# Rearranging the first microseconds of a fused attention and feed-forward kernel: smaller first tiles, weight loads meant to start earlier, split q, more engines for the casts

## The chip, the cores and the metric

The kernel runs on one core of a Trainium2 chip. The metric is the device time of that core in microseconds (us). Engines are written PE or TensorE (matrix products), PEld (its weight loads), DVE or VectorE, ACT or ScalarE, POOL or GpSimd, SP or SyncE. L603 means line 603 of the kernel in question; the changed kernel is some twenty lines longer, so the same statement has another number there.

## The reference

```python
# q, k, v: [8 batches, 8 heads, 576 tokens, 64]
phi(x) = concat(relu(x) * cos(theta_s), relu(x) * sin(theta_s))
kv  = einsum('bhsf,bhsd->bhfd', phi(k), v);   z = sum over s of phi(k)
num = einsum('bhsf,bhfd->bhsd', phi(q), kv);  den = einsum('bhsf,bhf->bhs', phi(q), z) + 1e-6
x = (num / den) as [4608 tokens, 512]
h = x @ w_in          # 512 x 2048
out = (h * cos(h)) @ w_out   # 2048 x 512
```

All inputs and the output are float32; the products run in float16 with float32 sums.

## The kernel before

Each batch gives 512 tokens to one chunk (four tiles of 128), and the ninth chunk collects the remaining 8 x 64. A planner in the Python code, run when the kernel is built, lists every step with an estimated cost and picks an order for each engine by list scheduling and rounds of random search with a fixed seed. The order is then frozen: at run time an engine executes its list and waits on semaphores. The parts that the change and the argument touch:

```python
# loads of q, k, v: two transfers each, four and five tokens per partition
def load(b, nm, due, hs=(slice(0, H),)):
    m, n = raw[nm], b % 2
    for h in hs:
        ...
        def go5(h=h, five=five):
            nc.sync.dma_start(out=blocks(m, n)[:, h], in_=five)          # partitions 2p + n
        def go4(h=h, four=four):
            nc.sync.dma_start(out=blocks(m, 1 - n)[:, h, 0:NT, :], in_=four)  # partitions 2p + 1 - n
        pl.add("SP", 0.65, 0, due, go4, (), [(x, 1 - n) for x in part], ...)  # issued first
        pl.add("SP", 0.65, 0, due, go5, (), [(x, n) for x in part], ...)      # issued second

# weight loads start only when k of batch 0 has landed: a tiny copy writes into w_in's tile
def weights():
    def hold():
        nc.gpsimd.tensor_copy(
            out=w_in_sb[0:1, 0, :].rearrange("p (g f) -> p g f", g=4)[:, :, 0],
            in_=raw[ORDER0[1]][0:1, 0, 0, 0:1].broadcast_to((1, 4)))     # ORDER0[1] is "k"
    pl.add("POOL", 0.4, 0.5, 0, hold, hk(ORDER0[1]), [("w_in", g) for g in range(4)])
    for g in range(4):      # four quarters of w_in, then w_out, by GpSimd's DMA
        ...

# first layer of chunks 0 and 1: two output blocks x two token tiles in each task
if c < 2:
    for quarter in range(4):
        for hf in range(2):
            for jp in range(2):
                ...   # 8 matmuls of 256 columns, needs x tiles 2*hf and 2*hf + 1
                pe(2 * NCT, MMH, due, mm, xk[2 * hf:2 * hf + 2] + [("w_in", quarter)], [("M1", m)])
                gate(...)          # ScalarE: cos; VectorE: h * cos(h)

FAST1 = {3: 2, 4: 2, 5: 2, 6: 2, 7: 4, 8: 4}   # groups of the first layer with fewer products

def first_attention():
    warm(14, 6.5)                               # dummy matmuls
    for nm in ORDER0:                           # "qkv"; only v in head halves
        load(0, nm, 0, HALVES if nm == ORDER0[2] else (slice(0, H),))
    weights()
    ...                                         # q: relu, transposes
    warm(10, 2.5, [("TR", 0)])
    ...                                         # k: relu; v casts; kv
    for t in range(NT):
        num(0, t, 8 + t, PAIRS[t])
        x_pe(0, t, t, *BANKS[t], "ACT", 8 + t)  # transposes of x and ScalarE's copy
```

A dummy or filler matmul multiplies zeros and only keeps TensorE busy. Batch 1's loads of q, k and v, and the second half of w_out, queue behind w_in and the first half of w_out.

Of the kernel before, what the change touches and what calls it, by code (L numbers as in the profile page):

```python
# [17 lines left out]
class Plan:  # L18
# [10 lines left out]

    PASSES, ROUNDS = 12, 97  # L30

# [78 lines left out]
    def forward(self, key):  # L110
# [27 lines left out]
        def first(n, e, t):  # L138
            opts = st[n]["opts"]
            return len(opts) == 1 or all(  # L140
                t + opts[e][1] <= max(free[x], avail[n]) + o[1] for x, o in opts.items())
        rings, now = {r: [] for r in self.SHARE}, 0.0
# [118 lines left out]
def kernel(  # L261
# [88 lines left out]
    PAIRS = [(BANKS[0], BANKS[1]), (BANKS2[0], BANKS2[1]), None, (BANKS[2], BANKS[3])]  # L350
    PAIRS1 = (None, PAIRS[3])

    Q_PE, X_PE = (), range(1, 3)
    VCAST = ("DVE", "ACT")
    LAZY = 8.0
    LATE_BY, LATE_W = (0.0, 1.0, 3.0, 1.0), 0.6
    ORDER0, ORDER1, HOLDW, W_FIRST = "qkv", "kqv", 1, None
# [9 lines left out]
    def pe(n, cost, due, fn, rd, wr):  # L367
        pl.add("PE", n * cost, n * cost, due, fn, rd, wr)
# [54 lines left out]
    def cast_v(b, t, eng, due, hs=slice(0, H), nt=1):  # L423
        heads = range(H)[hs]
        out_, in_ = V1[:, t, hs, 0:D], raw["v"][:, hs, t, :]
        if nt > 1:
            out_ = V1[:, t:t + nt, :, 0:D].rearrange("p t h d -> p h t d")
            in_ = raw["v"][:, :, t:t + nt, :]
        rd, wr = hk("v", heads), [("V1", t + i, h) for h in heads for i in range(nt)]
        f = nt * len(heads) / H  # L430
        cost = {"DVE": 0.09 + 0.33 * f, "ACT": 0.12 + 0.5 * f, "POOL": 0.9}
        fn = {"ACT": lambda: nc.scalar.activation(out=out_, in_=in_, func=AF.Copy),  # L432
              "DVE": lambda: nc.vector.tensor_copy(out=out_, in_=in_),
              "POOL": lambda: nc.gpsimd.tensor_copy(out=out_, in_=in_)}
        either(due, {e: cost[e] for e in ([eng] if eng else VCAST)}, fn, rd, wr)

# [101 lines left out]

    def x_pe(b, t, n, bank, key, eng, due):
        dst, dkey = xdst(b, t)  # L540
        ps = bank.bitcast(F16)[:, 0:NCT * P].rearrange("p (c s) -> p c s", c=NCT)
        x2 = x16[n].rearrange("p h d -> p (h d)")

        def mm():
            for c in range(NCT):
                nc.tensor.matmul(ps[:, c, :], lhsT=x2[:, c * P:(c + 1) * P], rhs=IDENT,  # L546
                                 is_transpose=True)
        pe(NCT, MMT, due, mm, [("x16", n), "ID"], [key])
        if eng == "ACT":
            act(0.5, due, lambda: nc.scalar.activation(out=dst, in_=ps, func=AF.Copy), [key], [dkey])  # L550
        else:
            dve(0.4, due, lambda: nc.vector.tensor_copy(out=dst, in_=ps), [key], [dkey])
# [10 lines left out]
    def mul(due, cost, fn, rd, wr, pool):  # L563

        if pool is None:
            dve(cost, due, lambda: fn(nc.vector), rd, wr)
        elif pool:
            pl.add("POOL", 0.1 + 2.1 * cost, 0.25 + 2.1 * cost, due, lambda: fn(nc.gpsimd), rd, wr,
                   port=True)
        else:  # L570
            dve(cost, due, lambda: fn(nc.vector), rd, wr, port=True)
# [11 lines left out]
    def layer1(c):  # L583
# [3 lines left out]
        if c < 2:  # L587
            n = 0
            for quarter in range(4):
                for hf in range(2):  # L590
# [50 lines left out]

    FAST1 = {3: 2, 4: 2, 5: 2, 6: 2, 7: 4, 8: 4}
    SUMS_AT = min(FAST1) - 1
# [315 lines left out]

    def warm(n, us, rd=()):  # L960
        def go():
            for i in range(n):
                nc.tensor.matmul(ATT[:, 0, :], lhsT=WZ[:, 0:P], rhs=WZ, start=True, stop=True)
        pl.add("PE", us, us, -1, go, rd, [("ATT", 0)])

    def weights():
        def hold():
            nc.gpsimd.tensor_copy(
                out=w_in_sb[0:1, 0, :].rearrange("p (g f) -> p g f", g=4)[:, :, 0],
                in_=raw[ORDER0[1]][0:1, 0, 0, 0:1].broadcast_to((1, 4)))  # L970
        pl.add("POOL", 0.4, 0.5, 0, hold, hk(ORDER0[1]), [("w_in", g) for g in range(4)])
        for g in range(4):
# [33 lines left out]
    def first_attention():  # L1006
# [4 lines left out]
        for nm in ORDER0:  # L1011
            load(0, nm, 0, HALVES if nm == ORDER0[2] else (slice(0, H),))
        weights()
        for t in range(NT):
            prep(0, "q", t, 0, "DVE", t)
            prep(0, "q", t, 1, "DVE" if t == 1 else "ACT", t)
            q_pe(0, t, *BANKS[t], "ACT" if t % 2 else "DVE", t)
        warm(10, 2.5, [("TR", 0)])
        for t in range(NT + 1):
            prep(0, "k", t, 0, "DVE", 4)  # L1020
            prep(0, "k", t, 1, "DVE" if t == 2 else "ACT", 4)
        for hb in range(2):
            for t in range(NT + 1):
                cast_v(0, t, "ACT" if t % 2 else "DVE", 5 + hb, HALVES[hb])
        kv(0, 7, BANKS2)
        for t in range(NT):
            num(0, t, 8 + t, PAIRS[t])
            x_pe(0, t, t, *BANKS[t], "ACT", 8 + t)

# [109 lines left out]
```

## Time and profile before

| | before |
|---|---|
| times of the first measurement | 283.74, 284.98, 285.03, and one of 722.17 us |
| profiled run (the one of 285.03), span | 283.2 us |
| TensorE busy | 270.7 us, 96% |
| first weight load issued | 11.21 us |
| last part of batch 1's v landed | 43.3 us |
| first layer of batch 1 begins (chain of waits) | 52.47 us |
| last block of 128 products begins | 264.74 us |

The run of 722.17 us is a lone outlier and is left out below. The last four rows are the ones to compare between kernels: they mark where the head ends and where the end is fixed. In the prediction are this kernel's totals, its slices and its timeline around 20 us. The chain of waits, followed back from the last instruction (start in us, length, what), adds the way there:

```profile
2.89 7.76 DMA km<-in_k_dram
...
15.98 0.44 DVE kvz L459
...
52.47 0.87 PE M L603 x8
...
264.74 14.11 PE M L896 x128
```

The reader sees one transfer in the head, k, and after 16.42 us (kvz copied) only the on-chip engines. No load of batch 1 stands on this chain. That is true, and I think it misled the prediction: a load that arrives just in time doesn't show on a chain.

### The profile page before, as it was taken

To read this page: it belongs to the slowest core of one execution; us is meant where nothing else is said; L and a number is where in the kernel's file an instruction comes from. 1 tells how busy PE (TensorE), PEld (TensorE's weight loads), DVE (VectorE), ACT (ScalarE), POOL (GpSimd) and SP (SyncE) were. 2 spreads that over 40 slices of the span, in tenths; PEclk is the share of its full clock that TensorE was granted. 3 is DMA by queue.
4 is the path that set the end of the run, shared out by engine and by line. 5 is a ranking of instruction groups with operands and counts; after the bars stand their busy time and mean duration, and the time that the engine had idled before them with its cause. 6 is when DMAs were issued, how large, how long until landed. Compare 5 with 4: busy or idle time off the path is not lost.

```text
span 283.2 us, 6709 instructions
## 1 busy us (share of the span) xinstructions
PE 270.7 (96%) x2652; PEld 213.6 (75%) x2652; DVE 253.0 (89%) x465; ACT 219.8 (78%) x374; POOL 38.5 (14%) x61
## 2 busy tenths in 40 slices
PE   7669999999999999999999999999999999999993
PEld 2457857677976678787878788868787888888882
DVE  2885798999999999999999999999999999999942
ACT  2944798888999999999999999998554748867610
POOL 1412110020100011001100200020002403331600
PEclk9986999999999999999999999999999999999999
DMA  6999999769998979996998799969032200300124
GB/s 211 304 205 274 254 300 319 243 176 269 270 307 165 316 114 355 247 267 161 285 258 220 170 280 260 242 200 154 0 58 93 87 9 3 148 2 0 68 83 148
DMA packets 77566, 53.29 MB, mean 188 GB/s; under 512 B 46048, under 2 KB 75232, under 8 KB 77536
## 3 DMA queue, kind: packets, MB, share of 16 engines
q1 hardware_dynamic: 70032, 39.73, 59.0%
q0 software_dynamic: 6784, 12.59, 16.8%
q10 hardware_dynamic: 720, 0.57, 0.6%
q8 instruction: 20, 0.33, 0.5%
q14 instruction: 10, 0.08, 0.1%
HBM read 36.74 MB, written 9.44 MB: 163 GB/s over the span
## 4 chain that ended last, share of the span: by engine, by line
PE 85%; DVE 8%; DMA 3%; issue 2%; ACT 1%; SPq 0%; DVEq 0%
PE M L896 32%; PE M L635 12%; PE M L739 11%; PE M L603 9%; PE M L833 5%; PE TR L739 5%; PE ATT L506 3%; PE ATT L445 3%; DMA km<-in_k_dram 3%; PE TR L635 2%; DVE KQ L419 2%; DVE gT L578 1%; DVE km L696 1%; PE M L546 1%; DVE S L878 1%
## 5 line engine op out<-in xcount | busy, mean ns | idle before, releaser
L896 PEld LDWEIGHTS <-gT 128*128 128x128 f16 x560 | 54.0, 98 | 8.4
L578 DVE TENSOR_TENSOR gT<-M,ch 128x512 f16<-128x512 f32 x78 | 51.9, 684 | 6.4 <-ACT ch L576 6.2
L896 PE MATMUL M<-w_out_sb,gT 128*128 128x256 f16 x448 | 56.1, 273 | 0.0
L576 ACT ACTIVATE ch<-M 128x512 f32<-128x512 f32 x80 | 46.7, 596 | 10.5 <-PE M L603 5.8
L418 ACT ACTIVATE KQ<-qm,CS 128x512 f16<-128x512 f32 x59 | 39.9, 721 | 4.4 <-DMA qm<-in_q_dram 4.4
L802 POOL DMA_DIRECT2D out_dram<-ost x32 | 17.6, 554 | 172.1 <-ACT ost L907 80.2
L635 PE MATMUL M<-xT,w_in_sb 128*128 128x512 f16 x160 | 39.0, 379 | 0.0
L418 ACT ACTIVATE KQ<-km,CS 128x512 f16<-128x512 f32 x54 | 37.1, 718 | 0.2 <-DMA km<-in_k_dram 0.2
L603 PE MATMUL M<-xT,w_in_sb 128*128 128x256 f16 x256 | 32.2, 283 | 1.2 <-ACT xT L550 0.7
L896 PE MATMUL M<-T,S 128*128 128x256 f16 x256 | 32.2, 273 | 0.0
L603 PEld LDWEIGHTS <-w_in_sb 128*128 128x128 f16 x256 | 25.7, 102 | 5.7 <-issue 1.8
L907 ACT ACTIVATE ost<-M 128x512 f32<-128x512 f32 x31 | 18.4, 594 | 14.8 <-PE M L896 14.7
L635 PEld LDWEIGHTS <-w_in_sb 128*128 128x128 f16 x192 | 18.2, 98 | 15.0
L896 PEld LDWEIGHTS <-S 128*128 128x128 f16 x256 | 24.9, 98 | 3.7 <-DVE S L878 0.2
L739 PEld LDWEIGHTS <-w_in_sb 128*128 128x128 f16 x240 | 23.0, 98 | 3.9 <-issue 0.2
L526 DVE TENSOR_TENSOR x<-ATT,rec 128x512 f16<-128x512 f32 x31 | 21.4, 691 | 1.1
L911 DVE TENSOR_TENSOR ost<-M,ost 128x512 f32<-128x512 f32 x24 | 16.4, 682 | 3.8 <-issue 3.6
L751 DVE TENSOR_TENSOR Z<-M,Z 128x512 f32<-128x512 f32 x26 | 17.4, 683 | 1.3 <-PE M L739 1.1
L506 PEld LDWEIGHTS <-qT 128*128 128x128 f16 x320 | 15.0, 98 | 4.7 <-issue 1.3
L878 DVE TENSOR_TENSOR S<-gT 128x2048 f16<-128x2048 f16 (+1 forms) x16 | 17.4, 1087 | 0.2
L739 PEld LDWEIGHTS <-WS 128*128 128x128 f16 x144 | 13.8, 98 | 2.4 <-issue 0.5
L432 ACT ACTIVATE V<-vm 128x1024 f16<-128x1024 f32 (+2 forms) x21 | 14.8, 739 | 0.0
(146 smaller groups left out, 461.8 us busy)
## 6 DMA issues: line engine op xcount, KB each, us to landing
out_dram<-ost POOLq DMA_DIRECT2D x32, 256.0 KB, 4.4
qm<-in_q_dram SPq DMA_DIRECT2D x8, 640.0 KB, 7.0
km<-in_k_dram SPq DMA_DIRECT2D x8, 640.0 KB, 6.2
qm<-in_q_dram SPq DMA_DIRECT2D x8, 512.0 KB, 5.9
km<-in_k_dram SPq DMA_DIRECT2D x8, 512.0 KB, 7.7
vm<-in_v_dram SPq DMA_DIRECT2D x6, 640.0 KB, 6.5
vm<-in_v_dram SPq DMA_DIRECT2D x6, 512.0 KB, 7.3
w_in_sb<-in_moe_w_in_dram POOLq DMA_DIRECT2D x4, 512.0 KB, 8.6
```

What stands on the lines that cost most here:

```text
L418: fn = {"ACT": lambda: nc.scalar.activation(out=out_, in_=in_, func=AF.Relu, scale=sc), "DVE": lambda: nc.vector.tensor_scalar(out=out_, i ...
L506: nc.tensor.matmul(bank[hb][:, hh * D1:(hh + 1) * D1], lhsT=a[:, h, :], rhs=z[:, h, :], start=(i == 0), stop=(i == len(parts) - 1))
L526: nc.vector.tensor_tensor(out=split(x16[n][:, hs, :], k), in0=A[:, :, :, 0:D], in1=split(rec[n][:, hs], k).unsqueeze(3).broadcast_to((P, k ...
L576: act(0.5, due, lambda: nc.scalar.activation(out=ch[c], in_=bank, func=AF.Sin, bias=math.pi / 2.0, scale=1.0), [key], [("ch", c)])
L578: mul(due, 0.61, lambda q: q.tensor_tensor(out=dst, in0=bank if len(dst.shape) == 2 else bank.rearrange("p (j s) -> p j s", j=dst.shape[1] ...
L603: nc.tensor.matmul(M1[m][:, jj * 2 * P:(jj + 1) * 2 * P], lhsT=w_in_sb[:, cc, j * P:(j + 1) * P], rhs=X[:, cc, ts], start=(cc == 0), stop= ...
L635: nc.tensor.matmul(M, lhsT=w_in_sb[:, cc, j * P:(j + 1) * P], rhs=X[:, cc, :], start=(cc == 0), stop=(cc == NCT - 1))
L739: nc.tensor.matmul(bank[0][:, j * TH:(j + 1) * TH], lhsT=a(cc, j), rhs=b[:, cc, :], start=(first and j == 0 and cc == 0), stop=(last and j ...
L802: pl.add(eng, 0.9 if eng == "POOL" else 0.65, 0, due, lambda: q.dma_start(out=dst, in_=src_), keys, [], dma=(nb, 355.0))
L878: dve(0.07 + 1.07 / NG, due, lambda: nc.vector.tensor_tensor(out=out_[:, sl], in0=a[:, sl], in1=b[:, sl], op=op), rd, wr, port=True)
L896: nc.tensor.matmul(bank[0][:, tt * MH:(tt + 1) * MH], lhsT=a[:, j, tt * P:(tt + 1) * P], rhs=b[:, j, :], start=(first and tt == 0 and j == 0),
L907: act(0.5, due, lambda: nc.scalar.activation(out=dst, in_=view(bank), func=AF.Copy), [bank[1]], dk)
```

## The change

The intent: begin the dense work sooner. The first layer of batch 0 starts by single token tiles; fillers keep TensorE's clock up meanwhile; the weight loads wait only for k's first part plus a short delay; q comes in head halves so that its preparation can begin early; v's casts may also go to GpSimd; and the last chunk uses two fast groups instead of four. The planner may now also choose the engine for batch 0's preparations of q and k and its casts of v, and has new cost estimates for GpSimd. Because the order is searched anew, every engine's order changes too. The diff cut to its core, without those choices and estimates:

```diff
-    PASSES, ROUNDS = 12, 97
+    PASSES, ROUNDS = 12, 117
...
+    PAIRS0, PAIRS1 = (None, PAIRS[1]), (None, PAIRS[3])
+    QV0 = "qv"
+    FILL = (4, 3, 2, 0)
-    VCAST = ("DVE", "ACT")
+    VCAST = ("DVE", "ACT", "POOL")
-    LATE_BY, LATE_W = (0.0, 1.0, 3.0, 1.0), 0.6
+    LATE_BY, LATE_W = (0.0, 1.0, 3.0, 2.5), 0.6
...
-            for quarter in range(4):
+            for t in range(NT if c == 0 else 0):
+                ...      # 16 matmuls of 128 columns on tile t, quarter 0 of w_in
+                pe(4 * NCT, MMT, due, mm, [xk[t], ("w_in", 0)], [("M1", m)])
+                gate(M1[m], ("M1", m), G[:, 0:4, ts], ...)
+            for quarter in range(1 if c == 0 else 0, 4):
...
-    FAST1 = {3: 2, 4: 2, 5: 2, 6: 2, 7: 4, 8: 4}
+    FAST1 = {3: 2, 4: 2, 5: 2, 6: 2, 7: 4, 8: 2}
...
+    HP = P // 2
...
-                out=w_in_sb[0:1, 0, :]...,  in_=raw[ORDER0[1]][0:1, 0, 0, 0:1]...)
-        pl.add("POOL", 0.4, 0.5, 0, hold, hk(ORDER0[1]), [("w_in", g) for g in range(4)])
+                out=w_in_sb[HP:HP + 1, 0, :]...,  in_=raw[ORDER0[1]][HP:HP + 1, 0, 0, 0:1]...)
+        pl.add("POOL", 0.4, 0.5, 0, hold, [((ORDER0[1], h), 1) for h in range(H)],
+               [("w_in", g) for g in range(4)])
+        for _ in range(2):
+            pl.add("POOL", 0.4, 0.5, 0, hold, [], [("w_in", g) for g in range(4)])
...
-            load(0, nm, 0, HALVES if nm == ORDER0[2] else (slice(0, H),))
+            load(0, nm, 0, HALVES if nm in QV0 else (slice(0, H),))
...
-        warm(10, 2.5, [("TR", 0)])
+        warm(16, 3.45, rd=[("TR", 0)])
...
-            num(0, t, 8 + t, PAIRS[t])
-            x_pe(0, t, t, *BANKS[t], "ACT", 8 + t)
+            num(0, t, 8 + t, PAIRS0[t % 2])
+            for _ in range(FILL[t]):
+                warm(1, 0.2157, M1[1], [(("ATT", "M2")[t % 2], 1)], [("M1", 1), ("fill", t)])
+            x_pe(0, t, t, *BANKS[3 - t % 2], "ACT", 8 + t, [("fill", t)])
```

More of the change, by code (lines that the diff above doesn't have):

```diff
@@ L140, in first @@
             return len(opts) == 1 or all(
-                t + opts[e][1] <= max(free[x], avail[n]) + o[1] for x, o in opts.items())
+                t + opts[e][1] <= at(n, x) + o[1] for x, o in opts.items())
         rings, now = {r: [] for r in self.SHARE}, 0.0
@@ L350 @@
     PAIRS = [(BANKS[0], BANKS[1]), (BANKS2[0], BANKS2[1]), None, (BANKS[2], BANKS[3])]
-    PAIRS1 = (None, PAIRS[3])
+    PAIRS0, PAIRS1 = (None, PAIRS[1]), (None, PAIRS[3])
+    QV0 = "qv"
+    FILL = (4, 3, 2, 0)
     Q_PE, X_PE = (), range(1, 3)
-    VCAST = ("DVE", "ACT")
+    VCAST = ("DVE", "ACT", "POOL")
     LAZY = 8.0
-    LATE_BY, LATE_W = (0.0, 1.0, 3.0, 1.0), 0.6
+    LATE_BY, LATE_W = (0.0, 1.0, 3.0, 2.5), 0.6
     ORDER0, ORDER1, HOLDW, W_FIRST = "qkv", "kqv", 1, None
@@ L430, in cast_v @@
         f = nt * len(heads) / H
-        cost = {"DVE": 0.09 + 0.33 * f, "ACT": 0.12 + 0.5 * f, "POOL": 0.9}
+        cost = {"DVE": 0.09 + 0.33 * f, "ACT": 0.12 + 0.5 * f, "POOL": 0.1 + 0.85 * f}
         fn = {"ACT": lambda: nc.scalar.activation(out=out_, in_=in_, func=AF.Copy),
@@ L537, in xdst, with x_pe @@
         return xR[:, :, i * P:(i + 1) * P], ("xR", i)
-    def x_pe(b, t, n, bank, key, eng, due):
+    def x_pe(b, t, n, bank, key, eng, due, after=()):
         dst, dkey = xdst(b, t)
@@ L547, in mm @@
                                  is_transpose=True)
-        pe(NCT, MMT, due, mm, [("x16", n), "ID"], [key])
+        pe(NCT, MMT, due, mm, [("x16", n), "ID", *after], [key])
         if eng == "ACT":
@@ L567, in mul @@
         elif pool:
-            pl.add("POOL", 0.1 + 2.1 * cost, 0.25 + 2.1 * cost, due, lambda: fn(nc.gpsimd), rd, wr,
+            pl.add("POOL", 3.4 * cost, 0.15 + 3.4 * cost, due, lambda: fn(nc.gpsimd), rd, wr,
                    port=True)
@@ L588, in layer1, with mm @@
             n = 0
-            for quarter in range(4):
+            for t in range(NT if c == 0 else 0):
+                m = m1n[0] % NM1
+                m1n[0] += 1
+                due = start[c] + n * width[c] / NJT
+                n += 1
+                ts = slice(t * P, (t + 1) * P)
+                def mm(m=m, ts=ts):
+                    for j in range(4):
+                        for cc in range(NCT):
+                            nc.tensor.matmul(
+                                M1[m][:, j * P:(j + 1) * P],
+                                lhsT=w_in_sb[:, cc, j * P:(j + 1) * P], rhs=X[:, cc, ts],
+                                start=(cc == 0), stop=(cc == NCT - 1))
+                pe(4 * NCT, MMT, due, mm, [xk[t], ("w_in", 0)], [("M1", m)])
+                gate(M1[m], ("M1", m), G[:, 0:4, ts], [("g", c, j, t) for j in range(4)], due + 1.5)
+            for quarter in range(1 if c == 0 else 0, 4):
                 for hf in range(2):
@@ L958, with warm @@
     wo = moe_w_out.rearrange("(j p) m -> p j m", p=P)
-    def warm(n, us, rd=()):
+    def warm(n, us, bank=ATT[:, 0, :], rd=(), wr=(("ATT", 0),)):
         def go():
             for i in range(n):
-                nc.tensor.matmul(ATT[:, 0, :], lhsT=WZ[:, 0:P], rhs=WZ, start=True, stop=True)
-        pl.add("PE", us, us, -1, go, rd, [("ATT", 0)])
+                nc.tensor.matmul(bank, lhsT=WZ[:, 0:P], rhs=WZ, start=True, stop=True)
+        pl.add("PE", us, us, -1, go, rd, wr)
+    HP = P // 2
     def weights():
@@ L968, in hold @@
             nc.gpsimd.tensor_copy(
-                out=w_in_sb[0:1, 0, :].rearrange("p (g f) -> p g f", g=4)[:, :, 0],
-                in_=raw[ORDER0[1]][0:1, 0, 0, 0:1].broadcast_to((1, 4)))
-        pl.add("POOL", 0.4, 0.5, 0, hold, hk(ORDER0[1]), [("w_in", g) for g in range(4)])
+                out=w_in_sb[HP:HP + 1, 0, :].rearrange("p (g f) -> p g f", g=4)[:, :, 0],
+                in_=raw[ORDER0[1]][HP:HP + 1, 0, 0, 0:1].broadcast_to((1, 4)))
+        pl.add("POOL", 0.4, 0.5, 0, hold, [((ORDER0[1], h), 1) for h in range(H)],
+               [("w_in", g) for g in range(4)])
+        for _ in range(2):
+            pl.add("POOL", 0.4, 0.5, 0, hold, [], [("w_in", g) for g in range(4)])
         for g in range(4):
@@ L1011, in first_attention @@
         for nm in ORDER0:
-            load(0, nm, 0, HALVES if nm == ORDER0[2] else (slice(0, H),))
+            load(0, nm, 0, HALVES if nm in QV0 else (slice(0, H),))
         weights()
         for t in range(NT):
-            prep(0, "q", t, 0, "DVE", t)
-            prep(0, "q", t, 1, "DVE" if t == 1 else "ACT", t)
+            for hs in HALVES:
+                for g in range(2):
+                    prep(0, "q", t, g, "", t, hs)
             q_pe(0, t, *BANKS[t], "ACT" if t % 2 else "DVE", t)
-        warm(10, 2.5, [("TR", 0)])
+        warm(16, 3.45, rd=[("TR", 0)])
         for t in range(NT + 1):
-            prep(0, "k", t, 0, "DVE", 4)
-            prep(0, "k", t, 1, "DVE" if t == 2 else "ACT", 4)
+            for g in range(2):
+                prep(0, "k", t, g, "", 4)
         for hb in range(2):
             for t in range(NT + 1):
-                cast_v(0, t, "ACT" if t % 2 else "DVE", 5 + hb, HALVES[hb])
+                cast_v(0, t, "", 5 + hb, HALVES[hb])
         kv(0, 7, BANKS2)
         for t in range(NT):
-            num(0, t, 8 + t, PAIRS[t])
-            x_pe(0, t, t, *BANKS[t], "ACT", 8 + t)
+            num(0, t, 8 + t, PAIRS0[t % 2])
+            for _ in range(FILL[t]):
+                warm(1, 0.2157, M1[1], [(("ATT", "M2")[t % 2], 1)], [("M1", 1), ("fill", t)])
+            x_pe(0, t, t, *BANKS[3 - t % 2], "ACT", 8 + t, [("fill", t)])
     def second_attention():
```

## The prediction

> **What bounds the kernel now.** I read the page first (totals, slices), then the chain of waits, then the engines by stage, then the timeline of TensorE and the DMA landings in the head.
>
> ```profile
> PE 270.7 (96%) x2652; PEld 213.6 (75%) x2652; DVE 253.0 (89%) x465; ACT 219.8 (78%) x374; POOL 38.5 (14%) x61
> ...
> PE   7669999999999999999999999999999999999993
> ...
> PEclk9986999999999999999999999999999999999999
> ```
>
> TensorE is busy in every slice but the first three and the last; its clock dips in the fourth. "Busy" is no proof of full use, so I added up work at the rates that dense runs show: 0.109 us for a matmul of 256 columns (8 in 0.87 us on the chain), 0.216 for 512, 0.057 for a transpose, about 0.031 for one of 65 columns. All real work comes to some 257 us; after 21.76 us, where the first layer of batch 0 begins, about 252 are left, and TensorE finishes at 278.87 us, 257 later. So only 5 us of that stretch are lost. The stages say where:
>
> ```profile
> 17.30:21.80 4.50, 1.95 (x20) 1.19 (x18) 3.78 (x15) 1.79 (x3) 0.43 (x3) 0.73 1.24 208
> ...
> 19.60:26.45 6.85, 5.49 (x34) 4.14 (x34) 3.34 (x11) 2.88 (x5) 2.02 (x4) 0.52 1.18 246
> ...
> 107.00:134.00 27.00, 27.00 (x287) 21.40 (x285) 25.81 (x48) 26.17 (x46) 0.66 (x2) 1.00 1.03 255
> ...
> 240.00:265.00 25.00, 25.00 (x231) 22.39 (x229) 24.66 (x36) 18.13 (x31) 8.61 (x9) 1.00 0.11 43
> ```
>
> The columns are length, busy time and count of TensorE, its weight loads, VectorE, ScalarE and GpSimd, then granted clock, DMA share and GB/s. From 107 to 134 us TensorE is full with VectorE and ScalarE at 96%: nothing to win there except by less work. Between 19.60 and 26.45 us the clock is half. The cause and cost show on TensorE's timeline:
>
> ```profile
> 17.78 0.61 PE L546 MATMUL M<-IDENT,x 128*128 128x128 f16 x4 [0.38 <-DVE x L526]
> 19.14 0.45 PE L546 MATMUL M<-IDENT,x 128*128 128x128 f16 x4 [0.75 <-DVE den L522]
> ...
> 20.46 0.62 PE L546 MATMUL M<-IDENT,x 128*128 128x128 f16 x4
> 21.76 1.87 PE L603 MATMUL M<-xT,w_in_sb 128*128 128x256 f16 x8 [0.69 <-ACT xT L550]
> 23.42 0.63 PE L546 MATMUL TR<-IDENT,x 128*128 128x128 f16 x4
> 23.85 3.93 PE L603 MATMUL M<-xT,w_in_sb 128*128 128x256 f16 x24
> ```
>
> The first layer's matmuls are twice two tiles wide, so the first can't start before two token tiles of x are transposed and copied, and finally starts at 21.76 us although tile 0 was in SBUF at 19.03 (ScalarE's copy at 18.43 plus 0.60). Its first eight take 1.87 us instead of 0.87. The half clock covers 21.76 to 26.44 us of dense work: 4.68 us at half rate, 2.3 us lost. The other 2.7 us of the 5 are small VectorE waits, chiefly at 33 to 39 us, where the chain alternates between gates and k preparations of batch 1.
>
> **What the Trainium skill says.** "TensorE: Matmul & The Clock Gate", Part 1, says that the clock is halved after an idle activity window of about 3.4 us and released after a busy one, and Part 4 that transposes don't count as activity in the same way. The trace agrees: between 17.4 and 21.76 us TensorE has nothing but 12 x transposes and four 65-column products, and is at half clock for 6.8 us, two such windows, from 19.6. "SBUF — State Buffer", Who interferes with whom, says that GpSimd shares a port pair with VectorE and one blocks the other for a whole instruction. In this trace GpSimd's 128x512 multiply takes 1.28 us in some places and 1.8 to 2.15 in others, which fits. "DMA: Bandwidth & Descriptors", Specifications, gives about 358 GB/s of HBM reading per core. Here, qkv of batch 0 (3.54 MB), w_in (4.19 as fp32), the first half of w_out (2.1), some 1.7 of the second half and qkv of batch 1 (3.54) are in by 43.3 us, 15 MB in 41.5 us: 360 GB/s. So the DMA has no room to spare in the head.
>
> **The change part by part.**
>
> *Single tiles.* Quarter 0 of the first layer of batch 0 (32 matmuls of 256 columns, 3.49 us) becomes four tasks of 16 matmuls of 128 columns (64 x 0.057 = 3.65 us), one per token tile. Now the four x tiles follow VectorE's normalisations, which begin once kvz is copied (16.42 us on the chain). Tile by tile: normalisation 1.05 us from the ATT bank, 1.27 from a pair of banks, transposes 0.45, copy 0.60. Tile 0 lands at about 19.05, then about 20.4, 21.4 and 22.7 us. TensorE takes 0.91 for each, so quarter 0 ends at about 23.6 us. Before, it ended at 27.78 us (where the chain passes to the late q transposes). Gain: 4.1 us at full clock; of these 2.3 are the clock and 1.8 the earlier start less waits between tiles.
>
> *Fillers.* Nine dummy matmuls of 512 columns (4, 3, 2, 0) run while VectorE normalises, and the dummy burst before k grows from 10 to 16. They are 1.9 and 1.3 us in idle time, cost nothing in themselves, and are what makes the clock part of the gain come true. New bank choices (ATT and the M2 pair for num, TR and M1_2 for x) leave M1_0 and M1_1 to the tiles.
>
> *Weights earlier.* They are held until k has landed whole:
>
> ```profile
> 10.71 0.19 POOL L968 CAST w_in_sb<-km 1x4 f16<-1x4 f32 x1 [9.23 <-DMA km<-in_k_dram]
> 11.21 3.52 POOL L974 DMA_DIRECT2D w_in_sb<-in_moe_w_in_dram  x4 [0.31 <-POOL w_in_sb L968]
> ```
>
> By the list of DMA issues with their times to landing, the first part of k was issued at 2.21 and landed 6.6 us later, at 8.8. Three holds of 0.19 and gaps of up to 0.3 put the first weight issue at about 10.0 to 10.4, 0.8 to 1.2 us earlier. The first quarter landed at 17.1 (11.2 + 5.9), the fourth about 27.4; both are earlier than the tiles need them even unchanged (19.05 and about 30.6 us). The value lies later: all of batch 1's loads move up by about 1 us.
>
> *q in halves.* q landed whole at 7.4 us; its first half should be usable near 5.3. But k lands at 10.65 either way (same bytes ahead of it), and the chain runs from there: k preparations 2.7 us on two engines, v casts, kv. So this gives about nothing on the path; it only moves two qT copies (0.68 VectorE, 1.02 ScalarE) out of 15.2 to 16.3.
>
> *v casts on GpSimd.* Batches 0 and 2 to 7 may use it. A 1024-column cast costs ScalarE 1.07 us and VectorE 0.68. Moving some of nine frees ScalarE a few us in stages where TensorE is the bound: 0, perhaps 0.3 us in the head.
>
> *Last first layer: two fast groups instead of four.* A fast group is 28 matmuls of 256 columns, 3.05 us; the plain one 16 of 512, 3.45. Two groups: +0.8 us TensorE, where it is full (240 to 265 us). VectorE spends 3 x 0.68 on additions, 1.22 on the double gate and 0.68 on the single one in a fast group (3.94 us), 4 x 0.68 = 2.72 in a plain one: 2.4 us less for two, in a stretch where it is at 98.6%; there, and at 215 to 228 us where the chain is all VectorE, waits of about 0.5 us may go. Net +0.3 us.
>
> Sum: -4.1 (tiles and clock) + 0.3 (last layer) = -3.8 us, before what batch 1 takes back.
>
> **The rivals.** *The head becomes DMA-bound.* With layer 1 of batch 0 done at 34 us instead of 39.6, TensorE has 2.3 us of q transposes and 6.9 us of second-layer halves (32 x 0.216) before it needs batch 1's v, whose last part landed at 43.3 us (now about 42.3), plus 4 us to casts, kv and x. It would stand from about 43 to 46.5. Before, at 52.3 us, it reached the first layer of batch 1 late because of that same filler work, so most of the gain survives; I charge 0 to 2 us. If it took it all back, the time would be 283 to 284. *The clock still drops.* The window is free-running and fillers of 2 us may be too few; then 2.3 us stay lost: 283. For it: the kv and num products run small; against: the longer burst ends nearer kv. *Earlier weights delay v.* Both share the engines; v's last part landed at 13.8 us, and the first weight packets came about 2 us after their issue, so the overlap is under 1 us; v late by 0.5 would pass straight through kv to tile 0: +0.5. *VectorE becomes the bound in the head*: between 7.5 and 53 us it is busy 37 of 45.5, and 4 us less leaves it at 89%: no.
>
> **Range and chances.** The two timed fast runs are 283.74 and 284.98, the profiled one 285.0: base 284.6. Minus 3.8, plus 0.3 for the DMA stall's likely share net of earlier loads: 281.0. All rivals mild gives 279.2; stall and clock together give 283.5. Under 278.9 (2%) needs more than the 5 us that the dense stretch loses at all, less the 0.8 added: 0.1. Slower by 2% would need a broken schedule: 0.01.
>
> **What would show it.** Right: first-layer matmuls of 128 columns from about 19 us, granted clock near 1.0 from 17 to 28 us, the last tile's task over by 23.7, first-layer end near 34.5; TensorE's end near 275 us with the final 4.3 us (last copy and store) unchanged. Wrong: clock still half after 19 us; v casts later than 15.1 us; TensorE waiting on w_out or batch 1's v at 42 to 48 us; a new wait on GpSimd casts; waits at 240 to 265 us larger than before.

## The result

The changed kernel took 287.57 us (median of four runs, 286.82 to 288.26); the kernel before 283.74, 284.98 and 285.03 in its fast runs. A ratio is the mean time of one kernel's fast runs over the mean of the other's in the same rounds, so it is not quite the ratio of the medians: here 1.0105, with a 95% interval of 1.0059 to 1.015. So the kernel became 1% slower. That is "within 2%", but 6.6 us above the predicted 281.0 and outside its range.

The profiled spans are 283.2 and 286.5 us. The page of the changed kernel:

```profile
PE 272.4 (95%) x2675; PEld 212.2 (74%) x2675; DVE 250.6 (87%) x462; ACT 214.5 (75%) x368; POOL 43.8 (15%) x70
...
PE   7679997999999999999999999999999999999993
...
PE 85%; DMA 8%; DVE 4%; SPq 1%; issue 0%; ACT 0%; DVEq 0%
```

The totals hardly differ, and every engine but GpSimd (14% before, 15% now) even has a little less of the span. Two places differ: TensorE has a "7" in its seventh slice (43 to 50 us), and the last line, the chain by engine, gives the DMA 8% where the kernel before had 3%. The chain says which transfers:

```profile
4.18 8.46 DMA km<-in_k_dram
...
18.25 0.44 DVE kvz L461
...
19.55 0.85 PE M L982 x2
20.63 1.28 PE M L982 x3
...
25.74 2.68 PE M L601 x48
...
31.74 14.21 DMA vm<-in_v_dram
46.04 0.70 DVE V L435 x3
...
54.99 1.77 PE M L621 x16
...
267.67 13.99 PE M L914 x128
```

k's second part now leaves SyncE at 4.18 us instead of 2.89, and ends the wait at 12.64 instead of 10.65. Fillers (L982) are on the chain. And between 31.74 and 45.95 us the chain is a transfer, batch 1's v. TensorE worked through most of that time and then stood 1.1 us for the cast of it. Against the kernel before, the first layer of batch 1 begins 2.52 us later, the last block of 128 products 2.93 us later; the rest of the 3.3 us is the last store, which took about 0.4 us longer. So nearly all of the loss was made in the first 55 us.

GpSimd's timeline shows the weight loads. The columns are start, length, engine, line, operation, tiles, shapes, count, and in brackets the idle time before and what ended it:

```profile
12.78 0.92 POOL L989 CAST w_in_sb<-km 1x4 f16<-1x4 f32 x3 [11.30 <-DMA km<-in_k_dram]
14.01 3.36 POOL L998 DMA_DIRECT2D w_in_sb<-in_moe_w_in_dram  x4 [0.31 <-POOL w_in_sb L989]
```

The "early" weight load was issued at 14.01 us, 2.8 us later than before. In the source the reason can be read. The hold reads partition row 64. In batch 0 the five-token transfer fills the even partitions and is issued second; the four-token transfer fills the odd ones and is issued first. Row 64 is even, so the copy depends on the second transfer. The planner was told that it reads part 1, the first transfer; that key is used for the order alone. The semaphore follows the data, and is the one of the second transfer. Then come two more holds: 0.92 us for the three together instead of 0.19 for one. The hold of the kernel before reads row 0, which is even as well: it too had waited for the second transfer, so the new hold released nothing sooner.

What that does to the DMA engines shows in stages. The columns are the stretch, its length, busy time and count of TensorE, its weight loads, VectorE, ScalarE and GpSimd, the granted clock, the DMA share and GB/s. First the kernel before, then the changed one:

```profile
13.50:16.50 3.00, 2.17 (x46) 1.79 (x47) 2.83 (x9) 2.43 (x6) 1.23 (x2) 1.00 1.07 170
```

```profile
13.50:16.50 3.00, 1.75 (x16) 0.78 (x15) 3.00 (x9) 3.00 (x7) 2.69 (x4) 1.00 0.23 35
```

For three microseconds the transfers are at 35 GB/s: only the rest of v is still landing (its last part was issued at 8.02 us and took 7.6, so it was in at 15.6 us, against 13.8 before), and the weights' first packets don't come before 15.8 us.

### The profile page after: what moved, and what is told of

Its sections match the earlier page's. It is cut to its first block, busy times and chain, and to the rows that moved or that the text cites. A ratio compares the mean times of both kernels' runs of the same rounds, so it can differ in the third digit from the quotient of the medians.

```text
span 286.5 us, 6736 instructions
## 1 busy us (share of the span) xinstructions
PE 272.4 (95%) x2675; PEld 212.2 (74%) x2675; DVE 250.6 (87%) x462; ACT 214.5 (75%) x368; POOL 43.8 (15%) x70
## 4 chain that ended last, share of the span: by engine, by line
PE 85%; DMA 8%; DVE 4%; SPq 1%; issue 0%; ACT 0%; DVEq 0%
PE M L914 34%; PE M L653 14%; PE M L757 10%; PE M L621 6%; DMA vm<-in_v_dram 5%; PE TR L757 4%; PE M L851 4%; PE ATT L508 3%; DMA km<-in_k_dram 3%; PE TR L653 3%; PE ATT L447 3%; DVE KQ L421 1%; PE M L601 1%; DVE V L435 1%; PE M L982 1%; PE M L548 1%
## 5 line engine op out<-in xcount | busy, mean ns | idle before, releaser
L578 ACT ACTIVATE ch<-M 128x512 f32<-128x512 f32 x85 | 49.8, 596 | 11.9 <-PE M L653 4.4
L914 PE MATMUL M<-w_out_sb,gT 128*128 128x256 f16 x448 | 55.4, 273 | 0.0
L420 ACT ACTIVATE KQ<-qm,CS 128x512 f16<-128x512 f32 (+1 forms) x63 | 40.9, 696 | 4.4 <-DMA qm<-in_q_dram 4.4
L653 PEld LDWEIGHTS <-w_in_sb 128*128 128x128 f16 x224 | 21.1, 98 | 17.8 <-issue 0.7
L621 PE MATMUL M<-xT,w_in_sb 128*128 128x256 f16 x224 | 26.8, 272 | 0.4 <-DVE gT L580 0.4
L621 PEld LDWEIGHTS <-w_in_sb 128*128 128x128 f16 x224 | 21.4, 98 | 3.5 <-issue 0.5
L757 PEld LDWEIGHTS <-w_in_sb 128*128 128x128 f16 x216 | 20.6, 98 | 4.1
L528 DVE TENSOR_TENSOR x<-ATT,rec 128x512 f16<-128x512 f32 x32 | 22.1, 691 | 1.1
L508 PEld LDWEIGHTS <-qT 128*128 128x128 f16 x320 | 15.9, 100 | 4.7 <-issue 1.7
L436 POOL CAST V<-vm 128x512 f16<-128x512 f32 (+1 forms) x9 | 7.6, 865 | 65.3 <-DMA vm<-in_v_dram 65.3
L508 PE MATMUL ATT<-kvz,qT 128*128 128x65 f16 x288 | 15.7, 195 | 0.5 <-DVE kvz L461 0.5
```

Source lines behind the costliest of these rows:

```text
L420: fn = {"ACT": lambda: nc.scalar.activation(out=out_, in_=in_, func=AF.Relu, scale=sc), "DVE": lambda: nc.vector.tensor_scalar(out=out_, i ...
L508: nc.tensor.matmul(bank[hb][:, hh * D1:(hh + 1) * D1], lhsT=a[:, h, :], rhs=z[:, h, :], start=(i == 0), stop=(i == len(parts) - 1))
L528: nc.vector.tensor_tensor(out=split(x16[n][:, hs, :], k), in0=A[:, :, :, 0:D], in1=split(rec[n][:, hs], k).unsqueeze(3).broadcast_to((P, k ...
L578: act(0.5, due, lambda: nc.scalar.activation(out=ch[c], in_=bank, func=AF.Sin, bias=math.pi / 2.0, scale=1.0), [key], [("ch", c)])
L621: nc.tensor.matmul(M1[m][:, jj * 2 * P:(jj + 1) * 2 * P], lhsT=w_in_sb[:, cc, j * P:(j + 1) * P], rhs=X[:, cc, ts], start=(cc == 0), stop= ...
L653: nc.tensor.matmul(M, lhsT=w_in_sb[:, cc, j * P:(j + 1) * P], rhs=X[:, cc, :], start=(cc == 0), stop=(cc == NCT - 1))
```

## The experiments

The first theory: the late weight loads carry the loss, in two steps (k late because q is in halves; the hold on the wrong part, three times), and everything that the tiles gain is hidden behind batch 1's loads. The rival: the new order, the fillers, the GpSimd casts or the last layer's two plain groups cost it. Runs e1 to e8 leave the planned order as it is and change only what is emitted, so the order is not a variable in them. All twelve results were correct. Each call shared the runs of the kernel before: medians 285.04 (7 runs), 285.41 (11) and 284.96 (11).

### e1_q_whole: q of batch 0 in whole heads again

```diff
+            if b == 0 and nm == "q":
+                if h == HALVES[1]: five = None          # go4 and go5 then emit nothing
+                else: h = slice(0, H); five, four = tokens(src[nm][b][h])
```

> The changed kernel with its plan and order frozen; only q of batch 0 is loaded whole (two transfers) instead of in halves (four). Theory A (the head is bound by the DMA: k of batch 0 landed at 12.7 us instead of 10.7 because of the halves, and the weights, held until k has landed, were issued at 14.0 instead of 11.2): k lands at 10.7 to 11.0, the first weight issue comes at about 12.1, batch 1's v lands about 2 us earlier (44 instead of 46), and the time falls by 1.5 to 2 us, to about 285.7. Theory B (the fillers at half clock ahead of the x transposes are the loss): k may land earlier, but the time stays within 0.5 us of 287.5. Theory C (the loss is in the newly planned middle and end, not in the head): 287.5 too.

285.57 us (285.4 to 287.18), ratio 1.0016 (0.995 to 1.0082): the loss is gone within the error. The first weight load was issued at 11.78 us, 2.2 us earlier than in the changed kernel. In this profiled run the clock was half from 8.65 to 15.48 us by the view of stages, and the longer burst of dummies stood on the chain, for the most part at that rate:

```profile
12.68 4.90 PE ATT L993 x16
...
52.56 1.77 PE M L632 x16
```

All the same the first layer of batch 1 began at 52.56, as in the kernel before (52.47). A burst that is free at full clock is not free at half clock, but here even that was hidden.

### e2_first_part: k's two transfers in the other order

```diff
+            if b == 0 and nm == "k":
+                go4, go5 = go5, go4
```

The row that the hold reads now belongs to the transfer issued first; q stays in halves and the three holds stay.

> The changed kernel, order frozen; the two parts of k of batch 0 are issued in the other order, so that the row which the hold reads belongs to the part that is issued first. Theory A: the hold is released near 10.8 us instead of 12.8, the first weight issue comes near 12.0 instead of 14.0, the stretch from 13.5 to 16.2 us in which the DMA engines stand idle shrinks to under 1 us, batch 1's loads come 1.5 to 2 us earlier, and the time falls by 1.2 to 2 us, although k itself still lands at 12.7 and x of batch 0 is no earlier. Theories B and C: no change beyond 0.5 us.

285.59 us (285.44 to 286.21), ratio 1.0008 (0.9947 to 1.007).

```profile
10.18 0.71 POOL L991 CAST w_in_sb<-km 1x4 f16<-1x4 f32 x3 [8.71 <-DMA km<-in_k_dram]
11.19 3.65 POOL L1000 DMA_DIRECT2D w_in_sb<-in_moe_w_in_dram  x4 [0.31 <-POOL w_in_sb L991]
```

The hold is released at 10.18 instead of 12.78 us and the first weight load issued at 11.19. With one swapped pair the whole loss goes, within the error. But it went in e1 too, where the hold is still on the wrong part and q is whole. So neither error alone makes a loss that can be measured; both together put the weights at 14.01 us. And with weights as early as in the kernel before there is still no gain.

### e3_loads_as_before: q whole and one hold

```diff
 # and e1's edit
         for _ in range(2):
-            pl.add("POOL", 0.4, 0.5, 0, hold, [], [("w_in", g) for g in range(4)])
+            pl.add("POOL", 0.4, 0.5, 0, lambda: None, [], [("w_in", g) for g in range(4)])
```

> The changed kernel, order frozen, with q of batch 0 whole and a single hold instead of three, so that the loads of the head are those of the kernel before, while single tiles, fillers, casts on GpSimd and the plan stay. Theory A: k at 10.7, first weight issue at 11.3, batch 1's v at 43.5, and the time is that of the kernel before within 1 us (284 to 286). Theory B: 287 (fillers still there). Theory C: 287.

285.1 us (285.01 to 286.47), ratio 1.0001 (0.9925 to 1.0078): no difference from the kernel before that these runs could show (the interval is 0.8% each way, some 2 us). This is the run that isolates the tiles, the fillers and the new order from the loads: weights issued at 11.16 us, batch 1's v landed at 43.23 (11.21 and 43.3 before), clock full throughout. Its chain:

```profile
22.86 2.68 PE M L612 x48
...
30.47 12.76 DMA vm<-in_v_dram
...
52.26 1.77 PE M L632 x16
...
264.96 13.99 PE M L925 x128
```

And TensorE's timeline, where the second layer of batch 0 begins and where kv of batch 1 goes on:

```profile
36.81 3.62 PE L862 MATMUL M<-w_out_sb,gT 128*128 128x512 f16 x16
...
43.87 0.95 PE L458 MATMUL ATT<-V,KQ 128*128 128x65 f16 x20 [1.27 <-DVE V L446]
```

The corresponding steps in the kernel before:

```profile
39.42 3.62 PE L833 MATMUL M<-w_out_sb,gT 128*128 128x512 f16 x16
...
45.28 0.65 PE L445 MATMUL ATT<-V,KQ 128*128 128x65 f16 x16 [0.17 <-DVE V L433]
```

The second layer of batch 0 began at 36.81 us; in the kernel before, the same step began at 39.42. TensorE was 2.6 us ahead. Six microseconds later it stood 1.27 us for a v cast, whose v had landed at 43.23, and the first layer of batch 1 began at 52.26 against 52.47. The lead was real in this profile and 0.2 us of it survived.

### e4_no_fill: the changed kernel without its nine fillers

```diff
-                warm(1, 0.2157, M1[1], ...
+                warm(0, 0.2157, M1[1], ...
```

> The changed kernel, order frozen, without the nine filler matmuls. Theory B: the x transposes of tile 0 come 1.4 us earlier (20.5 instead of 21.9), quarter 0 of the first layer ends 1 to 1.5 us earlier, and the time falls by as much, unless the clock then stays at half for longer (6.8 us instead of 3.4). Theory A: quarter 0 may end earlier, but TensorE waits just as long for batch 1's v at 46 us, and the time stays within 0.4 us of 287.5.

287.57 us (287.01 to 288.44), ratio 1.0076 (1.0012 to 1.014): the same median as with them. The half clock lasted from 18.28 to 25.11 us (6.83 us), with them from 18.39 to 21.80 (3.41 us), and the mean granted clock of its four runs was 0.984 to 0.988, against 0.990 to 1.0 with them. So in this pair the fillers do hold up the clock (e5 and e7, with and without, overlap: 0.984 to 0.997 and 0.982 to 0.998), and it buys no time here: batch 1's v decides. This run is also the control for e1 to e3: it keeps both errors, ran in the same rounds, and none of its runs was under 287.01 us. Quarter 0 ended at 27.99 us, 0.4 before the changed kernel's 28.42, but k had landed 0.7 us earlier in this profile.

### e5_wout_after_v: e3, and w_out's second half held until batch 1's v is in

```diff
 # and e3's edits; in the hold of w_out's second half
-                in_=raw[nm][0:1, 0, 0, 0:1].broadcast_to((1, 2)))
+                in_=raw["v"][0:1, HB, 0, 0:1].broadcast_to((1, 2)))
```

If v is late because the DMA is full, then taking 2.1 MB of w_out from in front of it should free the tiles' gain.

> The kernel of e3 (the changed one with the loads of before), order frozen; in addition the second half of w_out is held until the second half of batch 1's v has begun to land, instead of until q has landed. In e3 TensorE was 2.6 us ahead of the kernel before at 36.8 us and lost all of it waiting for v (landed 43.2), which shared the DMA engines with the second half of w_out from 35 us on. If the DMA order is what takes the gain back, v lands 2 to 3 us earlier (about 40.5), kv of batch 1 goes through without a wait, and the time falls by 1.5 to 2.5 us under both kernels, to 282.6 to 283.6. If TensorE instead waits for w_out later (its second half is first used at about 54 us), or something else holds the first layer of batch 1, the time stays at 285.

285.09 us (284.15 to 286.02), ratio 0.999 (0.9963 to 1.0017), expected 282.6 to 283.6: a miss. The first half of the mechanism held: v landed at 41.4 us, and kv of batch 1 went on without a wait:

```profile
43.02 0.81 PE L458 MATMUL ATT<-V,KQ 128*128 128x65 f16 x20
```

The first layer of batch 1 began at 51.24 us, 1.0 us before e3's, and the last block at 264.00. From 37.4 to 51 us TensorE now had hardly a wait (0.35 us, for a copy of ScalarE). So the profile shows about 1 us where 1.5 to 2.5 were expected, it was the fastest of the six runs, and 1 us is no more than runs of one kernel differ by. Its head also ran 0.6 us later than e3's (second layer of batch 0 at 37.40 us). From that step to batch 1's first layer it took 13.84 us, in e3 15.45 and in the kernel before 13.05: without v's wait 1.6 us go. The other 0.8 are mostly the new order: eight products of 65 columns and four transposes more come before that step, an estimated 0.5 us.

### e6_before_wout_after_v: the same hold in the kernel before

The edit is e5's last two lines, on the kernel before.

> The kernel before, order frozen, with the same new hold alone. There TensorE reached batch 1's kv at 43.8 us and waited only 0.2 us for a v cast, so an earlier v is of no use to it: 285.0 within 0.7 us. If it gains as much as e5 does, the gain of e5 is that of the DMA order alone and the single tiles have no share in it.

286.0 us (285.73 to 288.58), ratio 1.0039 (1.0006 to 1.0072). That is 0.6 us above the 285.41 of the shared runs and just outside the expected 284.3 to 285.7. The kernel before gains nothing from an earlier v (41.7 us instead of 43.3) and is a little slower. Its profiled run was its slowest, 288.58 us, so I don't place the loss; the later w_out is a guess.

### e7_wout_nofill and e8_wout_first_part: e5 without fillers, and e5 with e2's swap

> e5 without the nine fillers. If the fillers hold the clock up in runs in which the DMA doesn't hide it, quarter 0 ends 1 to 2.3 us later without them and the time rises by about 1 us over e5; if they only stand in front of the x transposes (1.3 us with the clock at full rate), it falls by 0.5 to 1 us. Where both are true they cancel.

284.53 us (283.95 to 286.81), ratio 0.998 (0.9947 to 1.0014).

> e5 with the two parts of k of batch 0 swapped, so that the weights are really released by the first part that is issued, with one hold: first weight issue near 9.3 us instead of 11.2. The DMA gap at 13 to 14.5 us closes and everything after it in the queue comes up to 1 us earlier; but the first weight packets now run beside v of batch 0, whose last part landed at 13.8. If that delays the v casts (v at 14.5 or later), kv and x of batch 0 come 0.5 to 1 us later and the gain is lost: 0 to +0.5 us against e5. If not: -0.5 to -1 us.

284.87 us (284.5 to 285.54), ratio 0.9985 (0.9962 to 1.0008). In e8 the weights left at 11.05 us instead of the expected 9.3, no more than 0.7 earlier than in e5: the one hold took 0.96 us here. Neither differs from the kernel before beyond its interval, and neither expectation is decided. The six runs of e7 show what such a difference drowns in: 286.81 and 286.6 us at a granted clock of 0.982, and 283.95, 284.28, 284.45 and 284.6 at 0.991 to 0.998. Within these six, the two groups are 2.4 us apart on average, and time goes with clock. It need not: the changed kernel took 287.64 us at 1.000 and 286.82 at 0.993.

### e9_new_plan_fast4, e10_new_plan, e11_new_plan_no_fill: planned anew with the load errors mended

So far the order had been made for loads that came otherwise. These three let the planner search again: q whole, k's five-token part issued first and the plan told so, one hold, w_out's second half after v. e9 has four fast groups in the last chunk, e10 two, e11 is e9 without fillers.

```diff
-    QV0 = "qv"
+    QV0 = "v"
...
-    ORDER0, ORDER1, HOLDW, W_FIRST = "qkv", "kqv", 1, None
+    ORDER0, ORDER1, HOLDW, W_FIRST = "qkv", "kqv", 2, None      # w_out waits for v, not q
...
+            both = [(go4, 1 - n, NT), (go5, n, NT + 1)]
+            for go, i, nt in both[::-1] if b == 0 and nm == "k" else both:
...
-        pl.add("POOL", 0.4, 0.5, 0, hold, [((ORDER0[1], h), 1) for h in range(H)],
+        pl.add("POOL", 0.4, 0.5, 0, hold, [((ORDER0[1], h), 0) for h in range(H)],
...
-        for _ in range(2):
+        for _ in range(0):
...
-                in_=raw[nm][0:1, 0, 0, 0:1].broadcast_to((1, 2)))
+                in_=raw[nm][0:1, HB, 0, 0:1].broadcast_to((1, 2)))
```

> A version meant to beat both, planned anew: single tiles and fillers kept; q of batch 0 whole; k's parts issued so that the one that the hold reads comes first, and the plan told so; one hold; the second half of w_out after batch 1's v; four fast groups in the last first layer, as before. If the DMA order was all that stood against the tiles, layer 1 of batch 1 begins near 50 us (52.4 before) and the time is 282 to 283.5. If new plans alone scatter the time by a microsecond or more, it may be anywhere from 283 to 286.

285.37 us (284.46 to 285.94), ratio 1.0007 (0.9978 to 1.0036).

> e9 with two fast groups in the last first layer, as the change has it. My count says +0.8 us of TensorE work and about half of it won back from VectorE waits: 0.3 to 0.8 us slower than e9. If the page's 98.6% busy VectorE in that stretch was the true bound, it is faster than e9 by up to 1 us.

285.26 us (284.8 to 287.37), ratio 1.0024 (0.9989 to 1.0059).

> e9 without fillers, planned so. In e7 the runs without fillers had the clock at 0.99 or more in four of six; there the fillers bought nothing. If so here, 0 to 0.7 us faster than e9, with single runs 2 us slower whose mean clock is near 0.98.

284.8 us (283.49 to 285.25), ratio 0.9987 (0.9955 to 1.002). None beats the kernel before, and e9's 282 to 283.5 did not come. In e9 the first layer of batch 1 began at 50.84 us by the chain, 1.6 us before the kernel before, and later steps gave it back, among them a wait of 1.0 us of TensorE for a ScalarE copy. Four or two fast groups can't be told apart between e9 and e10: the medians are 0.1 us apart, the means 0.5. e11 lies 0.6 us below e9, as expected without fillers, but within the error.

### e12_after_fast4: the changed kernel with four fast groups in the last chunk

```diff
-    FAST1 = {3: 2, 4: 2, 5: 2, 6: 2, 7: 4, 8: 2}
+    FAST1 = {3: 2, 4: 2, 5: 2, 6: 2, 7: 4, 8: 4}
```

> The changed kernel with four fast groups in the last first layer, and nothing else, which plans anew. If the loss of the change is in the head's loads, this stays at 287 to 287.6 (287.57 less 0.3 to 0.8). If the two fast groups given up were the loss, it falls to 285.

290.03 us (288.65 to 291.22), ratio 1.0176 (1.0134 to 1.0217): 2.5 us above the changed kernel's median, and no theory's number. The new search gave an order in which TensorE waits near the end:

```profile
240.00:265.00 25.00, 23.60 (x215) 20.77 (x214) 24.02 (x35) 16.80 (x28) 9.63 (x8) 1.00 0.12 44
265.00:279.00 14.00, 12.72 (x117) 11.10 (x116) 11.96 (x17) 6.27 (x10) 4.01 (x5) 1.00 0.19 75
```

It is 1.4 us idle in the first stretch and 1.3 in the second; the changed kernel with two groups is idle 0.55 us in the first and not at all in the second. At the very end ScalarE then waited 3.3 us for an output store to land, and the last matmuls ended at 284.75 us instead of 281.66. What two fast groups instead of four are worth stays open: a new plan moves the time by as much as the part that is tried. Had this run been my only test of the last layer, I would have credited the change there with 2.5 us, which e9 and e10 do not show.

## Why the prediction was wrong

First weight load, landing of batch 1's v, start of batch 1's first layer and of the last block, all in us from the profiled runs:

| kernel | weights | v landed | layer 1 of batch 1 | last block |
|---|---|---|---|---|
| before | 11.21 | 43.3 | 52.47 | 264.74 |
| changed | 14.01 | 45.95 | 54.99 | 267.67 |
| e1 | 11.78 | 42.2 | 52.56 | 265.24 |
| e2 | 11.19 | 43.16 | 52.20 | 264.88 |
| e3 | 11.16 | 43.23 | 52.26 | 264.96 |
| e4 | 13.34 | 45.05 | 54.09 | 266.78 |
| e5 | 11.73 | 41.4 | 51.24 | 264.00 |

In the kernel before, the changed one, e2, e3 and e4, v lands 31.7 to 32.1 us after the first weight load, whatever TensorE does meanwhile. In the changed kernel, e2, e3 and e4, batch 1's first layer follows 9.03 to 9.04 us after v. With the changed order the last block follows 212.7 to 212.8 us later in all six. So where v ends the wait, the time with this order is the issue of the weights plus constants. (In e1 v came 30.4 us after the weights; w_out's second half was issued at 35.93 us there and at 34.85 in e2, so probably more of it came behind v. There and in e5 v no longer ends the wait.)

**The weights.** "Three holds of 0.19 and gaps of up to 0.3 put the first weight issue at about 10.0 to 10.4." This step failed, and set the sign. It was 14.01, 2.8 us later than before instead of about 1 us earlier. The hold waited for the second part of k, as it had before; that part came later, so the hold began 2.07 us later (12.78 us instead of 10.71), and the three holds took 0.73 us more than the one. The swap of e2 takes the 2.8 us back in the profiled runs. (The number of holds is not all of the 0.73: a single one took 0.96 us in e8.) The intent was taken from the planner's key, and the partition of row 64 was not worked out from the two load functions, though both were in the source.

**q in halves.** "But k lands at 10.65 either way (same bytes ahead of it)" failed too; it was 12.64 us. The bytes are the same, the issues are not. SyncE's timeline, before and after, k's second part in the last line of each:

```profile
2.21 0.64 SPq L396 DMA_DIRECT2D km<-in_k_dram  x1
2.89 0.63 SPq L393 DMA_DIRECT2D km<-in_k_dram  x1
```

```profile
2.86 0.62 SPq L395 DMA_DIRECT2D qm<-in_q_dram  x1
3.52 0.62 SPq L398 DMA_DIRECT2D km<-in_k_dram  x1
4.18 0.63 SPq L395 DMA_DIRECT2D km<-in_k_dram  x1
```

An issue costs SyncE about 0.63 us for a half of q as for a whole part of k, so two more of them put k 1.3 us back in the queue. And the engines ran low meanwhile. The same stage of the kernel before, and of the changed one with a later stage beside it:

```profile
5.00:6.00 1.00, 1.00 (x4) 0.40 (x3) 0.00 (x0) 0.00 (x0) 0.00 (x0) 1.00 1.03 347
```

```profile
5.00:6.00 1.00, 1.00 (x6) 0.33 (x4) 0.73 (x3) 0.76 (x2) 0.00 (x0) 1.00 0.70 204
...
11.00:12.00 1.00, 1.00 (x11) 0.57 (x8) 0.80 (x2) 0.95 (x1) 0.00 (x0) 1.00 1.06 383
```

At 11 to 12 us halves of v, of the same size, move at 383 GB/s; so the size of a transfer alone is not it. That too little had been queued by 5 us fits both lines, but I only argue it. No run varies the time of issue alone. e1 and e3, with q whole, have k in at 10.5 to 10.7 us; e2 and e4, with halves, at 11.5 and 12.0. So with halves k came 0.8 to 2.1 us later. Such a landing scatters by itself: with the same loads the hold on k began at 10.61 us in e3's profile and at 11.17 in e5's.

**Single tiles.** "Gain: 4.1 us at full clock." The mechanism was right, the size off. From kvz to the end of quarter 0 I worked out 23.6 - 16.42 = 7.2 us. In e3, at full clock, it took 25.54 - 17.15 = 8.4, because tiles 1 to 3 ran as one block of 48 matmuls and not one by one: the transposes of the last tile waited 0.5 us for a bank that ScalarE was still copying. kvz also came 0.7 us later than in the kernel before. So 2.6 us were won by the start of the second layer, not 4.1. Most of these may be the clock: by the view of stages it was half from 19.36 to 26.20 us in the profile of the kernel before (the prediction's 19.60 to 26.45 reads 0.52 there, not 0.50), which makes an estimated 2.2 us of dense work lost, and it was full in e3's. The prediction's end of the first layer, "34 us instead of 39.6", also counts more than its 4.1 us: 39.6 - 4.1 is 35.5. It was 36.8.

**Where the 2.6 us went.** The rival "the head becomes DMA-bound" was named and charged with 0 to 2 us; e3 shows that it took nearly all, which the prediction had put at "283 to 284", although its own base with nothing gained was 284.6. I had computed 360 GB/s for the whole head and concluded that the DMA had no room (383 GB/s in the line above shows that this is no ceiling here), and then let most of the gain pass because TensorE in the kernel before "reached the first layer of batch 1 late because of that same filler work". That argument failed: v decides when that work can go on, and when v comes sooner (e5) the wait is gone. The chain of the kernel before shows no v there because TensorE arrived just as v did: its own wait for v's cast was 0.17 us.

**Fillers.** That they "cost nothing in themselves" was wrong in the changed kernel. Two groups were on its chain at half clock, 0.85 and 1.28 us, in front of the x transposes, which began at 21.88 us:

```profile
20.43 1.47 PE L982 MATMUL M<-S 128*128 128x512 f16 x3
```

The clock was also half for 3.4 us, so the rival "the clock still drops" half held. e4, e7 and e11 show that leaving the fillers out costs no time that could be measured.

**The last layer and the new plan.** Predicted +0.3 us. From batch 1's first layer to the last block the kernel before took 212.27 us and the changed one 212.68, +0.4. That is all parts after the head together, so that the two numbers are close proves nothing; e9, e10 and e12 could not split them.

**v casts on GpSimd.** Predicted 0 to 0.3 us, and none of them is on the chain. Four of its nine casts there, with busy time in us and mean of one in ns:

```profile
L436 POOL CAST V<-vm 128x1024 f16<-128x1024 f32 x4 | 4.7, 1182 | 25.5 <-DMA vm<-in_v_dram 25.5
```

The prediction's sentence on the port pair that GpSimd and VectorE share leaves out a condition of the page that it names (VectorE in a mode with two ports, or with two inputs from SBUF); nothing in its sum rests on it.

**The range.** It stood on 281.0, with 0.3 us charged for the stall on v. A check of the two load functions would have taken away the earlier weights, and nothing more: that k came 2 us later it would not have shown. Afterwards the rows above give 284.6 + 2.7 (v) + 0.4 (after the head) = 287.7 us with the gain hidden, and 287.57 was measured; that is a sum made with the result in hand. Three of the prediction's own signs of being wrong did appear: the clock half after 19 us, v casts later than 15.1 us (15.2 to 17.5), and TensorE waiting on batch 1's v at 42 to 48 us (1.1 us).

## What to carry to other kernels

Before counting a gain ahead of a full transfer queue, find the next load that the work needs and when it lands: a chain that shows no transfer may only mean that both arrive together. When a hold is moved to "the first part" of a load, work out which bytes it touches and which transfer writes them, since a scheduler's label binds nothing. And when a static order is searched anew, a difference near 1% may come from the search (e12), so test parts with the order frozen.

## What the Trainium skill lacked or had wrong

- "DMA: Bandwidth & Descriptors", Issuing engines are not separate DMA queues, calls the time that a sequencer takes to initiate a DMA "usually small relative to the DMA itself". Here an issue of q or k took SyncE 0.61 to 0.64 us (the very first 0.75), and a half part of q (256 KB) takes an estimated 0.73 us at the 358 GB/s that the same page gives under Specifications, or 0.68 at the 383 GB/s measured here from 11 to 12 us, which is above the page's figure. So the two are nearly equal. Splitting q put k's second issue back from 2.89 to 4.18 us and its landing from 10.65 to 12.64 (11.5 and 12.0 in e2 and e4). That transfers must also be queued some time ahead to keep the engines full would be worth a line there, if a test confirms it: 204 GB/s from 5 to 6 us against 347.
- "GPSIMD Engine Reference", 4.1 Engine selection, calls operations with one input "roughly line-rate" on GpSimd. The cast of 1024 columns from float32 to float16 took 1.18 us there; the prediction's figures for the same cast are 0.68 on VectorE and 1.07 on ScalarE. Beside VectorE that is 1.7 times as long, hardly less than the 1.9 times of the two-input multiply of 512 columns (1.28 us at best against 0.68).
- "TensorE: Matmul & The Clock Gate", Part 1, has the scatter of the warm-up between runs. It has no number for the mean granted clock of whole runs of one program: in e7 it was 0.982 in two runs and 0.991 to 0.998 in four, with times 2.4 us apart on average, 0.8%.
